# First tiles of a DFT kernel loaded in halves over two queues, with a shorter warm-up

## The chip, the cores and the metric

The kernel runs on one core of a Trainium2 chip. The core has five engines that run side by side, each with its own instruction stream: TensorE (matmuls, called PE in the profile; its weight loads are PEld), VectorE (DVE), ScalarE (ACT), GpSimd (POOL) and SyncE (SP). Loads from device memory are issued by an engine's queue, here SP's and ScalarE's, and carried by 16 DMA engines that all queues share. The metric is the device time of one execution in microseconds; 858.26 us is the median of three executions of the kernel before (858.01 to 858.42).

## The reference

For x of 2048 rows by 640 columns, the kernel mixes two results row by row with a gate g:

```python
g = sigmoid((x * gate_w).sum(-1, keepdims=True))
a = x @ dft_hid_re.T          # 2048 x 640
b = x @ dft_hid_im.T
A = dft_seq_re @ a - dft_seq_im @ b          # real part of the 2D DFT
h = x @ w1 + b1                              # 2048 x 1728
B = (h * tanh(softplus(h))) @ w2             # Mish
out = g * A + (1 - g) * B
```

All inputs and the output are 32-bit floats.

## The kernel before

The work is a long list of *steps*, written out when the kernel is built. A step loads tiles, prepares them, and runs matmuls on TensorE. Stages follow each other: the DFT along the sequence (`sq`), the DFT along the hidden dimension (`hd`), and the two dense products with Mish between them. Large products are cut into 2 by 2 blocks and done with seven block products in place of eight, so sums of tiles stand beside the matmuls.

Every 32-bit operand is split in two: a high part `h`, rounded to the format that TensorE reads fast, and a low part `l`, the rounding error. ScalarE makes the high part (`copy`, L144), VectorE the low part by a subtraction (`tt`, L141). A product is three matmuls: h with h, and each l with the other's h. All matmuls are issued in one helper (`mm`, L160).

The change touches the very start. The first stage multiplies c (`c_re`, a tile of 128 x 512, 256 KB, moving through TensorE) by x (`xn`, whose rows are stored in five blocks of 128 columns; the first three, a tile of 128 x 384 and 192 KB, are the weights here). Step 0 takes the first tile of each, c0 and x0, step 1 the second ones, and so on. Step 0 has its own preparation, `begin`, and its own order of matmuls, `products_by_part`:

```python
copy(wh, f[:, P:3 * P])                    # ScalarE: h of x0's blocks 1 and 2
for half in (LO, HI):
    nc.vector.tensor_copy(r[0][:, half], c[:, half])   # VectorE (L339): h of c0, by halves
tt(r[1], c, f32(r[0]), OP.subtract)        # VectorE: l of c0
tt(wl, f[:, P:3 * P], f32(wh), OP.subtract)
split(*part(w, 0, P), f[:, :P])            # h and l of x0's block 0
```

TensorE takes its matmuls in program order: c0's low half with x0's blocks 1 and 2, c0's high half with the same two, then all of c0 with block 0 (the *third product*), then the six with the low parts. ScalarE and VectorE are in order as well.

Loads of c and x are issued by the main loop on SP's queue (L1469), up to several steps ahead; tiles come from a pool of buffers (`FS`). Three things stand ahead of the loop: the loads of x0 and x1, issued on ScalarE's queue (L1351, L1353), the load of ScalarE's function table (L1354), and a warm-up of TensorE: `WARM` = 8 matmuls of 512 columns on a constant of ones, and one of 256 columns, whose results are not used. Each DMA tells of its landing through one of eight semaphores in turn, so an issue that takes a semaphore again waits for the landing of the DMA that had it.

Of the kernel before, what the change touches and what calls it, by code (L numbers as in the profile page):

```python
# [13 lines left out]
P = 128  # L14
# [5 lines left out]
FR = F - FC * P  # L20
NF = FC + 1
FP = 6
WARM = 8
EARLY = 3
LEAD = 8
LEAD_D = 5
# [80 lines left out]
def fnet_mish_gate(ctx: ExitStack, tc: tile.TileContext, xn, xt, c_re, c_im, wd_re, wd_im,  # L107
                   w1a, w1b, b1a, b1b, w2, gw, out):
    nc = tc.nc
# [48 lines left out]
    def mm(ps, a, b, start, stop):  # L158
        clock["pe"] += MM * ps.shape[-1] / N
        nc.tensor.matmul(ps, a, b, start=start, stop=stop, skip_group_check=True)  # L160
# [15 lines left out]
    LO, HI = slice(0, N // 2), slice(N // 2, N)  # L176
# [5 lines left out]
    def flush():  # L182
        while pend:
            pend.pop(0)()
# [38 lines left out]
    def job_load(i):  # L223
        j = jobs.pop(0)
        loaded.append((j, j.load(), i))

    def job_start():
        j, a, _ = loaded.pop(0)
        running.append((j.key, j.work(*a)))

    def job_go():
        key, work = running[0]
        pause = next(work, None)
        if pause is None:
            running.pop()
            done_jobs.add(key)
        return pause or 0
# [1110 lines left out]
        return f  # L1348

    x0 = RAW["xa", 0] = FS.get()  # L1350
    nc.scalar.dma_start(x0[:, :3 * P], xn[0, :, :3 * P])  # L1351
    x1 = RAW["xa", 1] = FS.get()
    nc.scalar.dma_start(x1[:, :3 * P], xn[1, :, :3 * P])  # L1353
    nc.scalar.preload_act_table_set("sigmoid_and_others")  # L1354
    ones = nc.const_aps.tensor(1.0, [P, N], F32).bitcast(F32R)
    for ps in psum.free[-WARM:]:
        mm(ps, ones[:, :P], ones, True, True)
# [94 lines left out]
    def spare(i, job=False):  # L1452

        return SPARE + (SPARE_D * job if i in narrow else (i >= n_dense) * SPARE_OUT) + sum(takes.get(i + j, 0) for j in range(5))

    li = ready = 0
    wait_until = 0
    for i in range(n_all):
        clock["step"] = i
        while ready < n_all and ready <= i + (LEAD_D if ready in narrow else LEAD):  # L1460
            while li < len(loads) and loads[li][0] <= ready + (AHEAD_D if loads[li][0] in narrow else AHEAD):
                n, (key, src) = loads[li]
                if n > ready and len(FS.free) <= spare(i):
                    break
                if id(src) in unwritten:
                    assert n > ready
                    break
                f = RAW[key] = FS.get()
                nc.sync.dma_start(f[:src.shape[0], :src.shape[1]], src)  # L1469
                li += 1  # L1470
            for prep in steps[ready][1]:
                prep()
            ready += 1
        clock["dve"] = max(clock["dve"], clock["pe"] - CREDIT)
        if not PEND or i + 1 not in narrow:
            flush()
        steps[i][2]()
        while stores and stores[0][3] <= i:
            dst, v, f, _ = stores.pop(0)
            nc.sync.dma_start(dst, v)  # L1480
            FS.put(f)
            unwritten.discard(id(dst))
        if steps[i][3]:
            steps[i][3]()
        for fn in events.get(i, ()):
            fn()
        if PEND == 1:
            flush()
        for r, w in list(extra) if i >= n_dense - BACK else ():
            if len(extra) > NB and any(r is o for o in R.free):  # L1490
                R.free = [o for o in R.free if o is not r]
                extra[:] = [e for e in extra if e[0] is not r]
                W.put(w)
        if i == 20:
            nc.sync.dma_start(b1s[:, :FC], b1a)
            nc.sync.dma_start(b1s[:FR, FC:], b1b)
        if not (jobs or loaded or running):
            while FX.free:
                FS.put(FX.get()[:, :N])
        while clock["dve"] < clock["pe"] + (SLACK_D if nd <= i < nm + D_END else SLACK if ("seq", "low", KH - 1) in done_jobs else SLACK_UP) and i >= wait_until and i not in quiet:  # L1500
            if running:
                wait_until = i + job_go()
            elif loaded and loaded[0][2] + (5 if i in narrow else 3) <= i and len(W.free) >= loaded[0][0].w:
                job_start()
            else:
                break
        while i not in no_load and jobs and len(loaded) < (NLOAD if i in narrow else 2) and len(FX.free) >= jobs[0].fx and i >= jobs[0].first and (i in narrow and not jobs[0].fs or len(FS.free) >= jobs[0].fs + spare(i, True)):
            job_load(i)
        if PEND == 2:
            flush()  # L1510
# [48 lines left out]
```

## Time and profile before

| | |
|---|---|
| median of three executions | 858.26 us (858.01 to 858.42) |
| the profiled execution, its own time | 857.84 us |
| its span, first to last instruction | 855.9 us |
| TensorE busy | 851.3 us, 99% of the span |
| VectorE, ScalarE busy | 87%, 59% |
| read from and written to device memory | 189.70 MB and 51.92 MB |

The page gives each engine's busy time. The chain of waits follows the work that ended last back to its start, and says at each step what released it. The timeline shows instructions in order of time: start, duration, engine, line, operation, output and inputs, and in brackets how long the engine was idle before and what ended that. A row of several merged instructions carries their number (x3). Names such as f, wh, rh and ps are the kernel's tiles: f for loaded tiles, rh and rl for the two parts of c, wh and wl for those of x, ps for accumulators.

### The profile page before, as it was taken

What the parts mean: (1) busy time and instruction counts of PE and PEld (TensorE: products, weight loads), DVE (VectorE), ACT (ScalarE), POOL (GpSimd) and SP (SyncE); (2) the same over time, 40 slices, a digit from 0 to 9 for tenths busy, and PEclk for the clock granted to TensorE, in tenths of its full rate; (3) what the DMA queues carried; (4) which work ended last, traced back from release to release, by engine and by line L of the source; (5) the groups of instructions that cost most, each with busy time, mean ns of one, the idle gap of its engine ahead of it and who ended that gap; (6) DMA issues with size and microseconds to landing.
All of it is one profiled execution on the core that took longest, in us unless ns stands there. A gap on an engine that the chain in (4) does not pass through costs nothing.

```text
span 855.9 us, 12423 instructions
## 1 busy us (share of the span) xinstructions
PE 851.3 (99%) x3748; PEld 704.3 (82%) x3748; DVE 742.0 (87%) x1320; ACT 507.0 (59%) x937; POOL 0.2 (0%) x4
## 2 busy tenths in 40 slices
PE   9999999999999999999999999999999999999998
PEld 7888888888888888888888888888888888888886
DVE  6999977999899869989898998877778889999991
ACT  6766646464555435757765665866867776542541
POOL 0000000000000000000000000000000000000000
PEclk9999999999999999999999999999999999999999
DMA  9975848594898999897677889999989997785942
GB/s 342 358 253 201 279 151 289 205 373 150 304 354 307 316 338 381 288 338 252 222 228 256 284 281 326 322 319 325 355 275 345 351 386 240 265 278 177 356 150 110
DMA packets 135602, 242.46 MB, mean 283 GB/s; under 512 B 15472, under 2 KB 22640, under 8 KB 135536
## 3 DMA queue, kind: packets, MB, share of 16 engines
q1 hardware_dynamic: 135104, 241.03, 82.0%
q8 instruction: 29, 0.48, 0.2%
q10 hardware_dynamic: 432, 0.66, 0.2%
q14 instruction: 37, 0.30, 0.1%
HBM read 189.70 MB, written 51.92 MB: 282 GB/s over the span
## 4 chain that ended last, share of the span: by engine, by line
PE 99%; DMA 0%; ACT 0%; issue 0%
PE ps L160 99%; DMA f<-in_xn_dram 0%; ACT f L144 0%; ACT wh L144 0%
## 5 line engine op out<-in xcount | busy, mean ns | idle before, releaser
L160 PE MATMUL ps<-rh,wh 128*128 128x512 f32 (+1 forms) x1029 | 398.7, 389 | 0.1
L160 PE MATMUL ps<-rl,wh 128*128 128x512 f32 x1017 | 394.7, 389 | 0.0
L160 PE MATMUL ps<-rh,wl 128*128 128x512 f32 x1016 | 394.3, 389 | 0.0
L144 ACT ACTIVATE rh<-f 128x512 fp32r<-128x512 f32 x420 | 255.5, 628 | 206.6 <-PE ps L160 101.3
L141 DVE TENSOR_TENSOR rl<-f,rh 128x512 fp32r<-128x512 f32 x419 | 281.5, 685 | 49.8 <-ACT rh L144 47.9
L141 DVE TENSOR_TENSOR f<-f,f 128x512 f32<-128x512 f32 (+2 forms) x342 | 218.6, 662 | 12.7 <-DMA u<-f 5.2
L160 PEld LDWEIGHTS ps<-rh,wh 128*128 128x128 f32 x1029 | 192.9, 188 | 40.6 <-ACT wh L144 0.6
L160 PEld LDWEIGHTS ps<-rl,wh 128*128 128x128 f32 x1017 | 190.9, 188 | 39.6
L160 PEld LDWEIGHTS ps<-rh,wl 128*128 128x128 f32 x1016 | 190.7, 188 | 39.5
L144 ACT ACTIVATE wh<-f 128x512 fp32r<-128x512 f32 (+3 forms) x201 | 91.8, 503 | 41.7 <-DVE f L141 33.7
L144 ACT ACTIVATE f<-ps 128x512 f32<-128x512 f32 (+1 forms) x135 | 77.2, 595 | 62.3 <-PE ps L160 52.4
L141 DVE TENSOR_TENSOR wl<-f,wh 128x512 fp32r<-128x512 f32 (+3 forms) x201 | 100.6, 535 | 9.8 <-ACT wh L144 9.4
L160 PE MATMUL ps<-wh,wh 128*128 128x512 f32 x232 | 90.3, 389 | 0.0
L160 PE MATMUL ps<-wh,wl 128*128 128x512 f32 x223 | 86.8, 389 | 0.0
L160 PE MATMUL ps<-wl,wh 128*128 128x512 f32 x222 | 86.4, 389 | 0.0
L141 DVE TENSOR_TENSOR f<-ps,f 128x512 f32<-128x512 f32 x98 | 63.5, 682 | 18.6 <-PE ps L160 17.9
L160 PEld LDWEIGHTS ps<-wh,wh 128*128 128x128 f32 x232 | 43.6, 188 | 9.1
L160 PEld LDWEIGHTS ps<-wh,wl 128*128 128x128 f32 x223 | 41.9, 188 | 8.7
L160 PEld LDWEIGHTS ps<-wl,wh 128*128 128x128 f32 x222 | 41.7, 188 | 8.6
L141 DVE TENSOR_TENSOR wl<-fx,wh 128x640 fp32r<-128x640 f32 (+2 forms) x43 | 28.4, 679 | 4.5 <-ACT wh L144 4.4
L144 ACT ACTIVATE wh<-fx 128x640 fp32r<-128x640 f32 (+4 forms) x46 | 27.5, 616 | 5.0 <-DVE fx L141 2.8
L141 DVE TENSOR_TENSOR f<-fx,f 128x256 f32<-128x256 f32 (+1 forms) x68 | 28.5, 442 | 1.5
(38 smaller groups left out, 171.0 us busy)
## 6 DMA issues: line engine op xcount, KB each, us to landing
f<-in_c_re_dram SPq DMA_DIRECT2D x128, 256.0 KB, 4.6
f<-in_c_im_dram SPq DMA_DIRECT2D x128, 256.0 KB, 5.0
f<-act SPq DMA_DIRECT2D x90, 256.0 KB, 4.9
f<-u SPq DMA_DIRECT2D x80, 256.0 KB, 3.8
f<-in_xt_dram SPq DMA_DIRECT2D x59, 256.0 KB, 4.8
act<-f SPq DMA_DIRECT2D x52, 256.0 KB, 4.2
u<-f SPq DMA_DIRECT2D x40, 256.0 KB, 4.5
f<-p SPq DMA_DIRECT2D x36, 256.0 KB, 4.6
```

Of the source, the lines that this page charges most:

```text
L141: nc.vector.tensor_tensor(o, a, b, op=op)
L144: nc.scalar.activation(o, a, AF.Copy, scale=scale)
L160: nc.tensor.matmul(ps, a, b, start=start, stop=stop, skip_group_check=True)
```

## The change

The warm-up loses one of its eight matmuls of 512 columns. c0 is loaded as two halves, the low one first on SP's queue, the high one second on ScalarE's. x0 is loaded as blocks 1 and 2, first on ScalarE's queue, and block 0, third there. x1 moves from ScalarE's queue to SP's, as its third load, behind c1. The table load stands behind ScalarE's three issues in place of two.

```diff
-WARM = 8
+WARM = 7
...
     x0 = RAW["xa", 0] = FS.get()
-    nc.scalar.dma_start(x0[:, :3 * P], xn[0, :, :3 * P])
+    nc.scalar.dma_start(x0[:, P:3 * P], xn[0, :, P:3 * P])
     x1 = RAW["xa", 1] = FS.get()
-    nc.scalar.dma_start(x1[:, :3 * P], xn[1, :, :3 * P])
-    nc.scalar.preload_act_table_set("sigmoid_and_others")
...
                 f = RAW[key] = FS.get()
-                nc.sync.dma_start(f[:src.shape[0], :src.shape[1]], src)
+                if li:
+                    nc.sync.dma_start(f[:src.shape[0], :src.shape[1]], src)
+                else:
+                    nc.sync.dma_start(f[:, LO], src[:, LO])
+                    nc.scalar.dma_start(f[:, HI], src[:, HI])
+                    nc.scalar.dma_start(x0[:, :P], xn[0, :, :P])
+                    nc.scalar.preload_act_table_set("sigmoid_and_others")
                 li += 1
+                if li == 2:
+                    nc.sync.dma_start(x1[:, :3 * P], xn[1, :, :3 * P])
```

Here `li` counts the loads of the list, so `li` = 0 is c0. ScalarE's stream at the start of the program, before; f_91 is x0, f_92 x1, f_93 c0, f_94 c1, f_95 c2 and f_96 x2, and DMAHWn is the n-th of the eight semaphores:

```order
L1351 DMA f_91<-in_xn_dram 128x384
L1353 DMA f_92<-in_xn_dram 128x384
L1354 ACT_TABLE_LOAD
L144 ACTIVATE wh_117<-f_91 128x256 [waits DMAHW0_49]
L144 ACTIVATE wh_117<-f_91 128x128
L144 ACTIVATE rh_75<-f_94 128x512 [waits DMAHW3_49]
L144 ACTIVATE wh_119<-f_92 128x384 [waits DMAHW2_49]
```

and the same place after the change:

```order
L1351 DMA f_91<-in_xn_dram 128x256
L1471 DMA f_93<-in_c_re_dram 128x256
L1472 DMA f_91<-in_xn_dram 128x128
L1473 ACT_TABLE_LOAD
L144 ACTIVATE wh_117<-f_91 128x256 [waits DMAHW0_49]
L144 ACTIVATE wh_117<-f_91 128x128 [waits DMAHW4_49]
L144 ACTIVATE rh_75<-f_94 128x512 [waits DMAHW3_49]
L144 ACTIVATE wh_119<-f_92 128x384 [waits DMAHW5_49]
```

The rounding of x0's block 0 (128x128), which had no wait of its own, now waits for a transfer of its own, and the roundings of c1 and x1 stand behind it. SP's queue at the start of the program, before:

```order
L1469 DMA f_93<-in_c_re_dram 128x512
L1469 DMA f_94<-in_c_re_dram 128x512
L1469 DMA f_95<-in_c_re_dram 128x512
L1469 DMA f_96<-in_xn_dram 128x384
L1469 DMA f_97<-in_c_re_dram 128x512
L1469 DMA f_98<-in_xn_dram 128x384
L1469 DMA f_99<-in_c_re_dram 128x512 [waits DMAHW0_49]
L1469 DMA f_100<-in_xn_dram 128x384 [waits DMAHW1_49]
L1469 DMA f_101<-in_c_re_dram 128x512 [waits DMAHW2_49]
```

and after the change:

```order
L1470 DMA f_93<-in_c_re_dram 128x256
L1468 DMA f_94<-in_c_re_dram 128x512
L1476 DMA f_92<-in_xn_dram 128x384
L1468 DMA f_95<-in_c_re_dram 128x512
L1468 DMA f_96<-in_xn_dram 128x384
L1468 DMA f_97<-in_c_re_dram 128x512 [waits DMAHW0_49]
L1468 DMA f_98<-in_xn_dram 128x384 [waits DMAHW1_49]
L1468 DMA f_99<-in_c_re_dram 128x512 [waits DMAHW2_49]
```

x1 (f_92) now stands third, c2 and all loads behind it one place later, and the first issue that waits for a landing is c3's (f_97) and no longer c4's (f_99). VectorE's stream changes in two waits: the cast of c0's high half and the subtraction for x0's block 0 each have a semaphore of their own now. TensorE's stream loses one warm-up matmul.

## The prediction

> **What bounds the kernel now.** I read the page's busy rows first, then the chain that ended last, then the first 8 us in order of time.
>
> ```profile
> PE 851.3 (99%) x3748; PEld 704.3 (82%) x3748; DVE 742.0 (87%) x1320; ACT 507.0 (59%) x937; POOL 0.2 (0%) x4
> ...
> PE 99%; DMA 0%; ACT 0%; issue 0%
> ```
>
> TensorE is busy for 851.3 of 855.9 us. Nothing that another engine does counts, unless it moves TensorE's start. The first pieces of the chain, in order of time, say where the start is set:
>
> ```profile
> 0.72 3.56 DMA f<-in_xn_dram
> 4.28 0.02 issue
> 4.31 0.43 ACT wh L144
> 4.73 0.04 issue
> 4.78 25.28 PE ps L160 x112
> ```
>
> x's first tile takes from 0.72 to 4.28 to land, ScalarE rounds two of its three blocks in 0.43, and from 4.78 TensorE runs matmuls without a gap (25.28 / 112 = 0.226 us each). All that this change can win or lose lies ahead of that. The same place in the timeline (start, duration, engine, line, what):
>
> ```profile
> 1.64 1.28 ACT L1354 ACT_TABLE_LOAD   x1 [1.64 <-PEq L1547]
> 4.12 0.29 DVE L339 CAST rh<-f 128x256 fp32r<-128x256 f32 x1 [4.12 <-DMA f<-in_c_re_dram]
> 4.63 0.29 ACT L144 ACTIVATE wh<-f 128x128 fp32r<-128x128 f32 x1
> 4.65 0.69 DVE L141 TENSOR_TENSOR rl<-f,rh 128x512 fp32r<-128x512 f32 x1
> 4.78 0.39 PE L160 MATMUL ps<-rh,wh 128*128 128x256 f32 x1
> 5.00 0.52 PE L160 MATMUL ps<-rh,wh 128*128 128x256 f32 x3
> 5.23 0.63 ACT L144 ACTIVATE rh<-f 128x512 fp32r<-128x512 f32 x1 [0.30 <-DMA f<-in_c_re_dram]
> 5.26 0.62 DVE L141 TENSOR_TENSOR wl<-f,wh 128x256 fp32r<-128x256 f32 x2
> 5.36 0.40 PE L160 MATMUL ps<-rh,wh 128*128 128x512 f32 x1
> 5.40 0.33 SPq L1469 DMA_DIRECT2D f<-in_c_re_dram  x1
> 5.59 0.39 PE L160 MATMUL ps<-rl,wh 128*128 128x512 f32 x1
> 5.76 0.51 ACT L144 ACTIVATE wh<-f 128x384 fp32r<-128x384 f32 x1
> 6.99 0.39 PE L160 MATMUL ps<-rh,wh 128*128 128x512 f32 x1
> 7.57 0.64 ACT L144 ACTIVATE rh<-f 128x512 fp32r<-128x512 f32 x1 [0.17 <-DMA f<-in_c_re_dram]
> ```
>
> c's first tile is there at about 4.10 (cast at 4.12) and its second at 5.21 (ScalarE starts at 5.23). x's second lands at about 5.38, for SP's issue at 5.40 waits on that transfer's semaphore. TensorE does four half matmuls from 4.78, the third product (x's block 0) at 5.36, and step 1 begins at 6.99. That third product is the row to watch: it needs x0[:, :P], which the change puts last on ScalarE's queue.
>
> **How fast the first bytes come.** The windows of the start (window, length, the five engines' busy time, granted clock, DMA share, GB/s), and the packets of each queue in 0.8 us of it (q1 is SP's, q10 ScalarE's):
>
> ```profile
> 1.50:2.50 1.00, 1.00 (x4) 0.82 (x3) 0.00 (x0) 0.86 (x1) 0.00 (x0) 1.00 0.71 95
> 2.50:3.00 0.50, 0.50 (x2) 0.36 (x2) 0.00 (x0) 0.43 (x1) 0.00 (x0) 1.00 0.87 313
> 3.00:3.50 0.50, 0.50 (x3) 0.38 (x2) 0.00 (x0) 0.00 (x0) 0.00 (x0) 1.00 1.05 398
> 3.50:4.00 0.50, 0.50 (x3) 0.41 (x2) 0.00 (x0) 0.00 (x0) 0.00 (x0) 1.00 1.06 403
> 4.00:4.40 0.40, 0.40 (x3) 0.23 (x1) 0.28 (x2) 0.09 (x1) 0.00 (x0) 1.00 1.06 405
> 4.40:4.80 0.40, 0.28 (x3) 0.03 (x1) 0.36 (x3) 0.40 (x2) 0.00 (x0) 1.00 1.12 342
> ...
> q1 hardware_dynamic: 111, 0.20, 64.6%
> q10 hardware_dynamic: 90, 0.12, 41.3%
> ```
>
> Added up, 95 kB have moved by 2.5, 252 by 3.0, 451 by 3.5, 652 by 4.0, 814 by 4.4 and 951 by 4.8. The engines are full from 3.0 on, so order decides. Between 3.5 and 4.3 the queues moved 111 and 90 packets, though q10's are 1.5 KB and q1's 2 KB: they take turns by packet, not by byte. The first pair of tiles (262 + 197 = 459 kB) is reached at 3.52, and lands at 4.10 (SP) and 4.28 (ScalarE); both pairs together (918 kB) at 4.70, landing at 5.21 and 5.38. From "moved" to "landed" is thus 0.5 to 0.6 us on SP's queue and 0.7 to 0.8 on ScalarE's.
>
> **The change part by part.** *Halves, by the same sums.* The first pair is now c0's low half and x0's blocks 1 and 2, 131 kB each: 262 kB at 3.03, landing at 3.6 and 3.80, half a microsecond earlier. Second on ScalarE's queue is c0's high half, and it takes turns with all of c1, which follows on SP: 128 packets beside 128, so it is through when 262 + 131 + 262 = 655 kB are, at 4.0, and lands at 4.77 instead of 4.10. Third is x0's block 0 (66 kB), beside x1 (197 kB): through at 918 kB, the same 4.70 as before, landing at 5.40 instead of 4.28. More packets for the same bytes add a little. Loads of 1 KB rows elsewhere show their price, against a stretch of 2 KB packets (q1 in 3 us around 414, and from 4.9 to 5.4):
>
> ```profile
> q1 hardware_dynamic: 576, 0.52, 58.9%
> ...
> q1 hardware_dynamic: 87, 0.17, 91.1%
> ```
>
> That is 0.589 x 16 x 3 / 576 = 49 ns, against 0.911 x 16 x 0.5 / 87 = 84 ns, so two halves cost 98 where one whole cost 84; with 8 rows for each DMA engine c0 takes 0.11 us longer, x0 about as much or less. x0's block 0 then lands at 5.5. The bounds are 5.4 (packets free) and 5.7 (0.2 for packets; and 0.1 if the slow packets up to 2.5 are no faster for being small, for then some 40 to 50 kB of the 95 are still to move, at 400 GB/s).
>
> *TensorE's start.* The wide rounding ends at 3.80 + 0.02 + 0.42, and the two low halves can start at 4.29, which is 0.49 earlier. That gain is not kept. The high half is cast from 4.79 to 5.08, its two matmuls start at about 5.13 and are over by 5.5. The third product waits for 5.5 + 0.02 + 0.29 (ScalarE's 128x128 row) + 0.05 (from 4.73 to 4.78, as now) + 0.10 (the first matmul after an empty pipe took 4.78 to 5.00, the next ones 0.12) = 5.96. Before it started at 5.36. **Sum: +0.60 us**, bounds +0.50 and +0.80; the early start is swallowed by the two waits behind it.
>
> *What stands behind the new wait.* TensorE takes its work in order, so all of step 0 is behind it. ScalarE too: c1's rounding waits behind block 0's, to 5.81 + 0.63 = 6.44, then x1's to 6.95; step 1 wants them at 6.99 + 0.60 = 7.59. VectorE: the rounding error of c0 comes at 5.08 + 0.69 = 5.8 (wanted 6.19), x0's two by 6.5 (wanted 6.88). So nothing else is late.
>
> *Half a microsecond less warm-up.* One matmul fewer at 0.43 (below) ends it at about 4.1 instead of 4.5. Taken at nothing: TensorE waits for data then anyway; the cover is the wait to 4.29. *Table load:* behind three issues instead of two (0.45 more) it runs from 2.09 to 3.37, 0.4 ahead of the first rounding: nothing. If it took over 0.4 longer, the low halves would start late, and still ahead of block 0. *SP's queue:* x1 takes the third place, c2 and all behind it move on by one, and c3's issue now waits for x0's landing (3.80; before it went at 2.58). c3 is wanted at 6.99 + 2 x 2.04 = 11.1 (nine matmuls of 0.226 a step), and it was there at 7.57, 3.5 us ahead; the issue moves by 1.2: nothing.
>
> [...]
>
> **Rivals.** *Turns by byte.* If small packets let ScalarE's queue through sooner, c0's high half is through at 524 kB (3.68, landing 4.45) and block 0 at 655 kB (4.0, landing 4.77); the third product starts at 5.23, 0.13 us earlier: 858.1. The 111 against 90 packets speak against it. Break-even is a landing of block 0 at about 4.9.
>
> *The half speed lasts longer.* Warm-up and end of the kernel:
>
> ```profile
> 3.03 1.06 PE L160 MATMUL ps<-const-float32-1.0 128*128 128x512 f32 x2
> 3.46 1.06 PE L160 MATMUL ps<-const-float32-1.0 128*128 128x512 f32 x2
> 3.89 0.77 PE L160 MATMUL ps<-const-float32-1.0 128*128 128x512 f32 x2
> ...
> 850.90:854.30 3.40, 1.33 (x6) 0.75 (x5) 0.00 (x0) 1.19 (x2) 0.00 (x0) 1.00 0.63 238
> 854.40:855.90 1.50, 0.00 (x0) 0.00 (x0) 0.00 (x0) 0.00 (x0) 0.00 (x0) 0.50 0.04 12
> ```
>
> Warm-up matmuls follow each other in 0.43 us, real ones of the same size in 0.23: TensorE runs at half speed at first, though the clock column reads 1.00 there, and it has full speed by 5.0, some 3.5 to 4.2 us after it began at 0.77. At the end, 3.4 us with 1.33 us of work took it to 0.50. After the change the work is broken from 4.1 to 4.29, from 4.65 to 5.13 and from 5.5 to 5.96. If these gaps make the count begin again at 5.96, half speed lasts 3.5 to 4.2 us longer and costs half of that, 1.75 to 2.1, beyond the 0.6: 860.6 to 861.0, slower by 0.3%. Against it speaks that the gap from about 4.5 to 4.78 did no harm, and that the work from 0.77 to 4.65 would be nine tenths busy. The mechanism decides from the point where the switch misses its place near 4.5. [...]
>
> **How the numbers follow.** The sum stands against the profiled execution, 857.84 us (855.9 and 1.9 around it), which gives 858.44; the median shown is 0.42 higher, and 858.26 + 0.60 gives 858.9. Late block 0: 0.70. Turns by byte, or anything that lands block 0 by 4.9: 0.16. Half speed lasting: 0.11. The rest, 0.03, is unexplained. The range goes from 858.26 - 0.13 - 0.25 (down to the lowest run) = 857.9 to 858.26 + 0.80 + 0.58 (from the profiled to the highest run) = 859.6, leaving out the half speed. 0.2% is 1.7 us, about what a measurement of this kernel can tell from no change. No start can win that much, as TensorE waits only until 4.78 and the clock's switch lies at 4.3 or later: faster 0.02. Slower is the half speed: 0.11. Same: 0.87.
>
> **What would show it.** Right: the chain of waits names x's block 0 on ScalarE's queue; the first real matmul is near 4.3, the third product near 6.0, step 1 near 7.6; ScalarE waits again for in_xn ahead of its 128x128 rounding. Wrong: the third product before 5.36 (turns by byte); real matmuls 0.43 apart after 6.0 (half speed); new idle time on TensorE behind 8 us (SP's order mattered after all).

## The result, and the profile after

The changed kernel takes 860.84 us (median of seven executions, 858.78 to 862.0), against 858.01 us (857.33 to 858.42, seven as well) for the kernel before. The ratio is 1.0033, with a 95% interval of 1.0021 to 1.0044: slower by a third of a percent. The profiled execution took 860.84 us, its span is 859.0, which is 3.1 more than before.

The busy row of the page after:

```profile
PE 852.9 (99%) x3747; PEld 705.4 (82%) x3747; DVE 742.5 (86%) x1320; ACT 507.6 (59%) x937; POOL 0.2 (0%) x4
```

TensorE is idle for 6.1 us in place of 4.6 (859.0 - 852.9, 855.9 - 851.3): 1.5 more. It is also busy for 1.6 us more, with one matmul fewer. So there are two losses: TensorE waits longer, and it works more slowly somewhere. The chain of waits of the kernel after, its first pieces (start, duration, what), shows where the first one is:

```profile
0.73 0.41 ACTq L1351
...
1.16 0.46 ACTq L1471
...
1.65 4.61 DMA f<-in_xn_dram
...
6.28 0.32 ACT wh L144
...
6.64 23.45 PE ps L160 x95
```

ScalarE's queue issues x0's blocks 1 and 2 (L1351), c0's high half (L1471), and then x0's block 0, which lands at 6.26, 4.61 us after its issue. ScalarE rounds it, and TensorE goes on at 6.64. The timeline of the same place:

```profile
3.24 0.29 DVE L339 CAST rh<-f 128x256 fp32r<-128x256 f32 x1 [3.24 <-DMA f<-in_c_re_dram]
3.43 0.42 ACT L144 ACTIVATE wh<-f 128x256 fp32r<-128x256 f32 x1
4.10 0.47 PE L160 MATMUL ps<-rh,wh 128*128 128x256 f32 x2
4.41 0.29 DVE L339 CAST rh<-f 128x256 fp32r<-128x256 f32 x1 [0.88 <-DMA f<-in_c_re_dram]
4.75 0.50 PE L160 MATMUL ps<-rh,wh 128*128 128x256 f32 x2 [0.18 <-DVE rh L339]
6.28 0.31 ACT L144 ACTIVATE wh<-f 128x128 fp32r<-128x128 f32 x1 [2.44 <-DMA f<-in_xn_dram]
6.50 0.62 ACT L144 ACTIVATE rh<-f 128x512 fp32r<-128x512 f32 x1
6.64 0.50 PE L160 MATMUL ps<-rh,wh 128*128 128x512 f32 x1 [1.39 <-ACT wh L144]
6.98 0.91 PE L160 MATMUL ps<-rl,wh 128*128 128x512 f32 x3
7.68 1.49 PE L160 MATMUL ps<-rh,wl 128*128 128x512 f32 x3
8.96 0.63 PE L160 MATMUL ps<-rh,wh 128*128 128x512 f32 x1
```

The first halves are there early, as they were meant to be: the cast of c0's low half at 3.24, the wide rounding of x0 at 3.43, the first real matmul at 4.10 in place of 4.78. Then TensorE waits 1.39 us for block 0. The third product starts at 6.64; before, it started at 5.36: 1.28 later. The last rows show the second loss. The three matmuls from 6.98 take 0.23 us each, from start to start ((7.68 - 6.98) / 3), and the three from 7.68 take 0.43 ((8.96 - 7.68) / 3). The windows of this stretch (window, length, busy time of TensorE, its weight loads, VectorE, ScalarE and GpSimd, the granted clock, DMA share, GB/s), after:

```profile
4.24:7.65 3.41, 1.84 (x9) 1.28 (x8) 2.12 (x5) 1.37 (x4) 0.00 (x0) 1.00 0.99 346
7.66:11.06 3.40, 3.40 (x9) 2.67 (x8) 3.40 (x8) 3.40 (x8) 0.00 (x0) 0.50 1.02 378
11.07:11.20 0.13, 0.13 (x2) 0.11 (x1) 0.13 (x1) 0.13 (x1) 0.00 (x0) 1.00 0.85 323
```

and before:

```profile
4.24:7.65 3.41, 3.29 (x16) 2.50 (x15) 3.37 (x9) 2.83 (x7) 0.00 (x0) 1.00 1.03 360
7.66:11.06 3.40, 3.40 (x16) 2.81 (x15) 2.84 (x6) 2.73 (x6) 0.00 (x0) 1.00 1.05 380
```

The trace's record of the granted clock begins at 4.24, with full speed; ahead of its first entry the column reads 1.00 too, although the warm-up matmuls there follow each other in 0.43 us and the real ones of the same size from 6.98 in 0.23. From 7.65 to 11.07 the record has 0.50, and then 1.00 again. TensorE does 9 matmuls in that time where it did 16. Half of 3.4 us is lost: 1.7. In the same length of time ahead of it TensorE had been busy for 1.84 of 3.41 us; before the change, for 3.29. Together 1.28 + 1.7 = 2.98 of the 3.1 us.

That is the profiled execution, and it doesn't stand for all of them. A stretch of 3.41 us at 0.50 lowers an execution's mean granted clock by 0.002. Of the six executions above 860 us, three have a mean of 0.997 or 0.998 (860.84, 861.05, 861.12). The other three (860.51, 860.59, 862.0) have 0.999 or 1.000, as the kernel before has: there the clock was not taken back. The experiments show a second way to lose the same time, full speed that comes late, at 10.23 to 13.22 in four profiles.

### The profile page after: what moved, and what is told of

It is laid out like the page before. It is cut to its first block, busy times and chain, and to the rows that moved or that the text cites. A ratio compares the mean times of both kernels' runs of the same rounds, so it can differ in the third digit from the quotient of the medians.

```text
span 859.0 us, 12424 instructions
## 1 busy us (share of the span) xinstructions
PE 852.9 (99%) x3747; PEld 705.4 (82%) x3747; DVE 742.5 (86%) x1320; ACT 507.6 (59%) x937; POOL 0.2 (0%) x4
## 4 chain that ended last, share of the span: by engine, by line
PE 99%; DMA 1%; ACT 0%; ACTq 0%; issue 0%
PE ps L160 99%; DMA f<-in_xn_dram 1%; ACT f L144 0%; ACTq L1471 0%; ACTq L1351 0%; ACT wh L144 0%
```

## The experiments

Two things had to be told apart: what takes the clock away (the gap in front of block 0, or the shorter warm-up), and why block 0 lands at 6.26 and not at 5.5. Of the fourteen kernels seven start from the changed kernel and seven from the kernel before. None leaves computation out; some add work whose result nobody reads, as said with each. The kernel before, run beside them, took 857.69 to 857.90 us (medians); each ratio is against it, and follows the means of all executions rather than the medians. The times given below at which full speed came are the first entries in the traces' records of the granted clock.

### The warm-up at its old length

```diff
-WARM = 7
+WARM = 8
```

> The changed kernel with the eighth warm-up matmul put back, all else as changed. Theory (late block, then the clock): block 0 of x's first tile still lands near 6.2, TensorE still stands idle for over 1 us ahead of the third product, and the clock still falls to half for some 3.4 us afterwards: 860.8, within 0.4. Rival (the shorter warm-up lost the clock): full speed is held from the start, and only the late block is left: about 859.1.

860.69 us (eleven executions), ratio 1.0023 (1.0014 to 1.0032). The executions fall into two groups with nothing between them: five from 858.72 to 858.82 and six from 860.69 to 861.14. The profiled execution, 858.81, is of the lower group. Its chain and two of its windows:

```profile
1.65 4.19 DMA f<-in_xn_dram
5.84 0.02 issue
...
6.22 5.97 PE ps L160 x25
```

```profile
2.90:6.32 3.42, 2.94 (x10) 2.20 (x9) 1.73 (x5) 1.39 (x4) 0.00 (x0) 1.00 1.03 375
...
6.32:9.73 3.41, 3.41 (x15) 2.86 (x16) 3.18 (x7) 3.41 (x8) 0.00 (x0) 1.00 1.06 388
```

In this execution block 0 landed at 5.84 and the third product started 0.86 late (6.22 - 5.36). Full speed came at 6.32 (10 matmuls in the first window, 15 in the second), it stayed, and 0.9 us were lost in all (858.81 - 857.90). So this group pays about what the late block costs. The upper one lies some 2 us higher, about the price of 3.4 us at half clock (1.7). No profile fell in it, but the mean granted clock of all six is 1.000. So the fall to half that I had expected happened in none of the eleven; that full speed came a stretch late in the six is argued from the distance and the clock. The changed kernel has the same two groups: 858.78 once, and six from 860.51 to 862.0. Five of eleven against one of seven is too few to say that the warm-up's length changes the odds. And with the old warm-up the median is as high, so the matmul that was taken out isn't needed for the jump.

### Warm-up matmuls in the gap

Six matmuls of 512 columns on the constant of ones, results not read, in front of the third product of the changed kernel:

```diff
+        if first:
+            pe = clock["pe"]
+            for _ in range(6):
+                mm(psum.free[-1], ones[:, :P], ones, True, True)
+            clock["pe"] = pe
```

> The changed kernel with six matmuls of 512 columns on ones, whose results nobody reads, put between the high half's matmuls and the third product; no load is touched. Theory (late block, then the clock): the third product stays at about 6.6, but TensorE is busy until it, the clock is not taken back, and real matmuls follow each other in 0.23 us from there on: 860.8 - 1.7 = 859.1. Rival (everything comes from waiting for data; the clock plays no part): 860.8, or a little more.

859.54 us (859.14 to 860.05, eleven executions), ratio 1.0018 (1.0009 to 1.0026). The timeline and two windows:

```profile
5.41 1.70 PE L160 MATMUL ps<-const-float32-1.0 128*128 128x512 f32 x6
...
6.94 0.40 PE L160 MATMUL ps<-rh,wh 128*128 128x512 f32 x1
7.18 0.86 PE L160 MATMUL ps<-rl,wh 128*128 128x512 f32 x3
```

```profile
4.40:7.60 3.20, 3.12 (x13) 2.50 (x13) 2.21 (x5) 1.45 (x4) 0.00 (x0) 1.00 1.02 365
7.70:11.00 3.30, 3.30 (x16) 2.73 (x15) 3.30 (x7) 3.29 (x8) 0.00 (x0) 1.00 1.02 361
```

The third product starts at 6.94, later than without the filling (6.64), and still the kernel is 1.3 us faster: full speed comes at 5.86 and stays, and no execution is above 860.05. More work in the gap costs less than the gap. This is the run that shows that the second loss hangs on TensorE's idle time.

### The same gap without any change of the loads

To have the gap alone: the kernel before, in which ScalarE rounds a constant, unread, ahead of x0's block 0. Three roundings in the first kernel, four in the last; the second has three roundings and the six matmuls of above in the gap.

```diff
+        for n in (N, N, P):
+            copy(psum.free[-2][:, :n], ones[:, :n].bitcast(F32))
```

> The kernel before with three roundings of a constant on ScalarE (128x512 twice, 128x128; results unread) ahead of the rounding of block 0. No load is changed; the third product is held up to about 6.4 to 6.9 as in the changed kernel. Theory (late block, then the clock): 1.1 to 1.6 us of waiting, and in most runs 1.7 us of half speed on top: 860 to 861.5 in the median. Rival (the loads themselves cost the rest of the 2.8 us): only the wait, 859.0 to 859.6 in all runs.

> As f2 with six matmuls on ones between the high half's matmuls and the third product. Theory: the wait stays, the clock is held: 859.0 to 859.7, in a narrow band. Rival (half speed comes from something else than TensorE's idle time): as f2.

> As the kernel with ScalarE held up by three roundings of a constant, with a fourth (128x512, 0.63 us). No load is changed; the third product moves from about 6.0 to about 6.6, as in the changed kernel, and TensorE's idle time ahead of it grows from 0.4 to about 1.0 to 1.2 us. Theory (a long enough gap loses the clock): the runs fall into two groups 1.7 to 2 us apart, near 859.2 and near 861, and more of them than 2 in 11 lie in the upper one. Rival (the clock is lost only where the loads are as in the changed kernel): one group near 859.2.

With three roundings the gap came out at only 0.42 us: the third product started at 6.01. 858.72 us, ratio 1.0015 (1.0006 to 1.0024); nine executions from 858.59 to 858.87, two at 860.46 and 860.49. The median I had expected is missed, since the gap was too short. Filled with matmuls the same kernel took 859.08 us (858.9 to 860.0), ratio 1.0016 (1.0007 to 1.0025): no execution jumped, but the median is 0.36 higher, so a gap this short wasn't worth filling. With four roundings it took 859.56, ratio 1.003 (1.0017 to 1.0042): four executions from 859.47 to 859.60, one at 860.8, one at 862.49. The profiled one is of the lower four. Its third product in the timeline, and two windows:

```profile
6.98 0.50 PE L160 MATMUL ps<-rh,wh 128*128 128x512 f32 x1 [1.09 <-ACT wh L144]
```

```profile
4.40:7.60 3.20, 2.11 (x9) 1.47 (x8) 1.56 (x5) 3.10 (x8) 0.00 (x0) 1.00 1.06 389
7.70:11.00 3.30, 3.30 (x17) 2.69 (x16) 3.30 (x7) 3.30 (x8) 0.00 (x0) 1.00 1.04 375
```

A gap of 1.09 us, nearly that of the changed kernel, and the clock stayed: full speed had come at 5.73, and in the 3.41 us from there TensorE was busy for 2.32. So a gap may bring the second loss, but needn't: 2 of 11 executions jumped in the kernel whose profile shows 0.42 us, 2 of 6 in the one with 1.09 us, none of 11 with the 0.42 filled, and 1 of the 118 executions of the kernel before (860.62). These counts are small. The jump, 1.7 us in the first kernel (860.48 - 858.72), needs no changed load. The mean clock of the four that jumped is 1.000, so full speed wasn't taken back in them; that it came late is argued, as no profile fell in them.

### Low parts ahead of block 0

The changed kernel, with step 0's matmuls in another order: the products of the low parts with blocks 1 and 2 go first, and the three of block 0 last, so that TensorE has work while block 0 is under way.

```diff
+        if first:
+            for n, c in ((0, l), (1, h)):
+                for ps, w in todo[:2]:
+                    mm(ps, w[n], c, False, False)
+            ps, w = todo[2]
+            for n, c, start in ((0, h, True), (0, l, False), (1, h, False)):
+                mm(ps, w[n], c, start, False)
+            return
```

> The changed kernel with step 0's matmuls in another order: the low parts of c and x with blocks 1 and 2 ahead of the three products with block 0, so that real work stands in the gap; loads as changed. Theory (late block, then the clock): the gap shrinks from 1.4 to 0.3 to 0.5 us, the clock is held, step 1 begins at 7.3 to 7.6 and not at 8.5 or later: 858.2 to 858.9 and no second group 1.7 us above. Rival (late loads cost in later steps too, whatever step 0 does): 860 or more.

859.33 us (858.36 to 860.5, eleven executions), ratio 1.0016 (1.0007 to 1.0025): 1.5 us better than the changed kernel, 0.4 above the expected range, and still not as good as the kernel before. In the profiled execution (860.49, among the highest) block 0 landed at 6.53 and held nobody up, but the matmuls were still at half speed at 7.6, as its timeline shows:

```profile
5.02 0.79 PE L160 MATMUL ps<-rh,wh 128*128 128x256 f32 x2 [0.29 <-DVE rh L339]
...
7.62 0.63 PE L160 MATMUL ps<-rh,wh 128*128 128x512 f32 x1
...
8.05 0.63 PE L160 MATMUL ps<-rl,wh 128*128 128x512 f32 x1
```

Full speed came only at 10.23 here, and was not taken back. The idle time left was 0.29 us ahead of c0's high half.

### The warm-up cut alone

The kernel before, with `WARM = 7`.

> The kernel before with WARM = 7, nothing else. Theory (late block, then the clock): the warm-up ends at 4.1, TensorE idles 0.7 us until 4.78, and the clock is held: 858.0, within 0.3. Rival (the shorter warm-up lost the clock): half speed lasts a window longer: about 859.7.

858.00 us (857.35 to 858.63, eleven executions), ratio 1.0000 (0.9991 to 1.0009). Nothing: the 1.7 us of one more stretch of 3.41 us at half speed are in no execution.

### Block 0 ahead of c0's high half

```diff
-                    nc.scalar.dma_start(f[:, HI], src[:, HI])
                     nc.scalar.dma_start(x0[:, :P], xn[0, :, :P])
+                    nc.scalar.dma_start(f[:, HI], src[:, HI])
```

> The changed kernel with the second and third issue on ScalarE's queue exchanged: block 0 of x's first tile ahead of c's high half. Theory (late block, then the clock): block 0 lands near 4.2, c's high half at 4.5 to 4.9, the third product starts at 5.2 to 5.5, no gap is over 0.6 us, the clock is held: 857.8 to 858.4. Rival (the shorter warm-up lost the clock): the order of loads gives back only the 1.3 us of waiting: about 859.6.

Missed by about 4 us: 862.03 (860.41 to 862.64, five executions), ratio 1.0047 (1.0034 to 1.006). Block 0 did land early, at 4.51. But c0's high half, now third, landed at 6.94. The chain, and the row of the timeline that waits for it:

```profile
1.66 5.28 DMA f<-in_c_re_dram
6.94 0.02 issue
```

```profile
7.32 1.23 PE L160 MATMUL ps<-rh,wh 128*128 128x256 f32 x3 [2.58 <-DVE rh L339]
...
10.90 1.48 PE L160 MATMUL ps<-rh,wh 128*128 128x512 f32 x3
12.18 1.04 PE L160 MATMUL ps<-rl,wh 128*128 128x512 f32 x3
13.06 0.39 PE L160 MATMUL ps<-rh,wl 128*128 128x512 f32 x1
```

So the place is slow, not the tile. The third load on SP's queue, x1, landed as late, at 6.76. With this gap of 2.58 us half speed lasted long: TensorE did 10 matmuls from 7.7 to 11.0, where the kernel before does 16. Here full speed was not taken back; it had not come yet. It came at 12.57: the three matmuls from 10.90 are 0.43 apart, those from 12.18 only 0.29. In two of the five executions (861.59, 862.03) the mean clock is 0.997, as in the changed kernel's profile, which speaks for a stretch taken back there.

### x1 one place later on SP's queue

In the changed kernel, `li == 3` in place of `li == 2`: x1 is loaded behind c2. This asks whether x1's bytes beside block 0 hold it up.

> The changed kernel with x's second tile one place later on SP's queue, behind c's third, so that block 0 has c's third tile beside it and not x's second. Theory P (the third place on ScalarE's queue is late whatever stands beside it): block 0 lands at 5.8 or later, the gap ahead of the third product is over 0.9 us, 860.5 within 0.5. Rival X (the rows of x's second tile are slow and hold block 0 up): block 0 lands by 5.6, the third product starts by 6.1, 858.8 to 859.5.

862.03 us (860.77 to 862.5, four executions), ratio 1.0044 (1.0029 to 1.0059). Block 0 landed at 6.71, and the third product waited 1.29 us for it, in the timeline:

```profile
7.10 0.79 PE L160 MATMUL ps<-rh,wh 128*128 128x512 f32 x1 [1.29 <-ACT wh L144]
```

Not earlier, but later. So x1's bytes beside it don't make block 0 late. The landing and the gap are as Theory P had them; the median is 1 us above its range, and in the profiled execution (862.5) full speed came only at 13.22.

### c0 on one queue, x0 on the other

Both halves of c0 on SP's queue, both parts of x0 and then x1 on ScalarE's, so that step 0 needs no third place. The second kernel has `WARM = 8` besides.

```diff
-                    nc.scalar.dma_start(f[:, HI], src[:, HI])
+                    nc.sync.dma_start(f[:, HI], src[:, HI])
                     nc.scalar.dma_start(x0[:, :P], xn[0, :, :P])
+                    nc.scalar.dma_start(x1[:, :3 * P], xn[1, :, :3 * P])
...
-                if li == 2:
-                    nc.sync.dma_start(x1[:, :3 * P], xn[1, :, :3 * P])
```

> Halves in the order of need: SP's queue carries c's first tile as low half and high half, ScalarE's carries x's first tile as blocks 1 and 2, then block 0, then x's second tile. Theory P: both second halves land in the second place of their queues, by 4.5, real matmuls begin at 3.9 and no gap is over 0.5 us; x's second tile, now in third place, lands at 5.4 to 6.2, and step 1 waits at most 0.5 us for it: 857.4 to 858.2, the kernel before or a little faster. Rival (any split into halves costs, by more and smaller packets): block 0 later than 5, 859 or more.

> As e6 with the eighth warm-up matmul put back. TensorE is in the warm-up until 4.3 to 4.5 and starts the real matmuls up to 0.4 us later at half speed, where 0.4 us is worth 0.2: 857.6 to 858.3, equal to e6 within 0.3. Rival (the warm-up length sets the clock): faster than e6 by 1 us or more in the median.

858.75 us (858.39 to 859.32) and 858.68 us (858.49 to 859.44), eleven executions each, ratios 1.0011 (1.0002 to 1.0019) and 1.001 (1.0001 to 1.0019). Better than the changed kernel by 2.1 us, and in no execution the jump; but the gain that I had expected didn't come. The halves were all there early (ScalarE's two roundings of x0 run from 3.62, and the second cast of c0 starts at 3.97), and then the third places were late again: c1 on SP's queue landed at 6.42, and step 1 waited. Of the first kernel's chain:

```profile
1.64 4.78 DMA f<-in_c_re_dram
...
7.54 4.60 PE ps L160 x19
```

Step 1 starts at 7.54, against 6.99 before: all the start gained, and 0.55 more, went to the third place. In the profile of the second kernel c1 landed at 7.43, and TensorE stood idle for 1.74 us ahead of step 1, the longest gap of all in which the clock stayed. Counted in steps of 3.41 us from the coming of full speed, which is an estimate, it lay across the end of a step, and in the two steps TensorE was busy for 2.26 and 2.82 us.

### c0 alone in halves

The kernel before, with c0 alone cut, its high half second on ScalarE's queue and x1 third there.

> The kernel before with only c's first tile in halves: the low one first on SP's queue, the high one second on ScalarE's; x's first tile whole and first, x's second third on ScalarE's queue, warm-up of eight and a half. Theory P: x's first tile lands at 3.7 to 4.1 whole, the high half by 4.7, both second at worst; the one in third place is x's second tile (5.5 to 6.3), which step 1 wants at 6.4: 857.8 to 858.6. Rival (the split of c, not block 0, costs): 859.5 or more.

858.82 us (858.24 to 860.0, eleven executions), ratio 1.0013 (1.0005 to 1.0022). Missed as well: x1, third, landed at 7.27, and step 1 started at 7.87 in the timeline:

```profile
7.87 0.96 PE L160 MATMUL ps<-rh,wh 128*128 128x512 f32 x3 [0.37 <-ACT wh L144]
```

### Is it the number of loads?

Two loads of 128 rows of 16 bytes, 4 KB together, unread, in the kernel before: in the first kernel both on ScalarE's queue between x0 and x1, in the second one at the head of each queue.

```diff
+    for i in range(2):
+        tiny = sb.tile([P, 4], F32, name=f"tiny{i}")
+        nc.scalar.dma_start(tiny, xn[2 + i, :, :4])
```

```diff
+    tiny = [sb.tile([P, 4], F32, name=f"tiny{i}") for i in range(2)]
+    nc.scalar.dma_start(tiny[0], xn[2, :, :4])
+    nc.sync.dma_start(tiny[1], xn[3, :, :4])
```

> The kernel before with two loads of 128 rows by 16 bytes (4 KB in all, into buffers that nobody reads) on ScalarE's queue between x's first and second tile. Theory C (what counts at the start is the number of loads, each of which takes its time to be set up, whatever its bytes): x's second tile, now the fourth load of its queue, lands 0.4 to 1.5 us later than 5.4, and DMA bandwidth dips between 3.5 and 5; 858.0 to 858.9. Rival (bytes and turns alone, as the prediction reckoned): it lands at 5.4 to 5.5, and the time is that of the kernel before within 0.2 us.

> The kernel before with one load of 128 rows by 16 bytes (into a buffer that nobody reads) ahead of everything on each of the two queues. Theory Q (each queue only needs its issue time): the first tiles land 0.45 us later, c's at about 4.2 to 4.55 and x's at 4.4 to 4.75, 858.2 to 858.5. Rival S (loads of both queues are set up one after the other, each taking some 0.4 us whatever its bytes): 0.8 us later or more, 858.6 to 859.

The first took 858.55 us (858.26 to 858.83), ratio 1.0008 (0.9998 to 1.0017). With 4 KB ahead of it, x1 landed at 6.74 in place of 5.38, and c2, on the other queue, at 5.68 in place of 6.18. x1's rounding in the timeline:

```profile
6.76 0.53 ACT L144 ACTIVATE wh<-f 128x384 fp32r<-128x384 f32 x1 [1.36 <-DMA f<-in_xn_dram]
```

So the queues take turns by packet even when one's packets hold 16 bytes: each of the 256 small rows let a row of 2 KB pass. Between 3.5 and 5.05 ScalarE's queue moved 279 packets (0.02 MB) and SP's 283 (0.50 MB). The 5.4 to 5.5 that the expectation gives for x1 was reckoned wrong; by turns x1 is through only when c0 and x0 (459 kB), c1 and c2 (262 each), and x1 with an equal load beside it (394) have moved. TensorE had no gap, and no execution jumped. In the profile full speed came at 6.68, and step 1 began at 7.69; how much of the 0.9 us over the kernel before is x1's stays open.

The second took 858.5 us, ratio 1.0014 (1.0005 to 1.0023), in two groups: six from 858.1 to 858.52 and four from 860.45 to 860.89. c0 landed at 4.71 and x0 at 4.88, against 4.10 and 4.28 in the profile before (and 3.65 and 3.85 in the earliest profile with the same loads, that of the three roundings). The profiled execution is the highest (860.89); its timeline:

```profile
5.37 1.65 PE L160 MATMUL ps<-rh,wh 128*128 128x256 f32 x5 [0.64 <-ACT wh L144]
6.82 1.48 PE L160 MATMUL ps<-rl,wh 128*128 128x512 f32 x3
8.10 1.48 PE L160 MATMUL ps<-rh,wl 128*128 128x512 f32 x3
```

A gap of 0.64 us in front of the first real matmul, and step 0 ran through at half speed ((8.10 - 6.82) / 3 = 0.43); full speed came at 10.24. The landings speak for a cost of each load at a queue's head, the lower group's times against a large one; the run doesn't settle it.

## Why the prediction was wrong

**The early start: right.** The chain names x's block 0 on ScalarE's queue, ScalarE waits for it ahead of its 128x128 rounding, and the early halves bring nothing. They came even earlier than said: the wide rounding started at 3.43 (3.80 + 0.02 in the working), c0's high half was cast at 4.41 (4.79). Both are 0.4 early. Most of that is the profile that the working stood on: in the five profiles with the loads of the kernel before, x0 lands between 3.85 and 4.28, and that one has the latest. Turns by byte would have brought block 0 early too, and it wasn't.

**Block 0's landing: right in kind, mis-sized.** The term was a landing at 5.5, bounds 5.4 and 5.7, and +0.60 us. Measured were 6.26 and +1.28; 5.84 and +0.86 with the long warm-up, 6.71 with x1 moved. The working took the engines as full from 3.0 on, and then only order decides. They weren't. The windows of the changed kernel:

```profile
3.50:4.00 0.50, 0.50 (x3) 0.40 (x2) 0.03 (x1) 0.35 (x1) 0.00 (x0) 1.00 1.23 262
4.00:4.40 0.40, 0.40 (x4) 0.37 (x2) 0.00 (x0) 0.00 (x0) 0.00 (x0) 1.00 0.63 173
4.40:4.80 0.40, 0.22 (x3) 0.05 (x1) 0.36 (x2) 0.00 (x0) 0.00 (x0) 1.00 0.93 222
4.80:5.20 0.40, 0.40 (x2) 0.25 (x2) 0.40 (x1) 0.00 (x0) 0.00 (x0) 1.00 0.77 275
```

Where the kernel before moved 403, 405, 342 and 332 GB/s, it is now 262, 173, 222 and 275: 234 kB less in 1.7 us, 0.6 us at 400 GB/s. The block was 0.76 later than said, so the sag would explain most of it, but not all: with the long warm-up the rate stayed at 365 or more over these windows, and the block was still 0.34 late. With c0 on one queue the sag is deepest, in the same view,

```profile
3.50:4.00 0.50, 0.50 (x3) 0.27 (x1) 0.24 (x2) 0.38 (x1) 0.00 (x0) 1.00 0.82 199
4.00:4.40 0.40, 0.38 (x3) 0.31 (x3) 0.37 (x2) 0.29 (x2) 0.00 (x0) 1.00 0.52 106
```

and with c0 alone cut there is none (397, 363, 353, 328 GB/s), though its third load came at 7.27. The sag is not the whole of it. The trace's packet records show what is behind the rest: every load there ends with 16 packets of 4 bytes, and it had landed 0.4 to 0.55 us after the last of them. For x0 in the kernel before these come between 3.27 and 3.79. For block 0 with the long warm-up fifteen come from 4.65 to 4.80, as the sum had it (moved at 4.70), and the last at 5.47; by then 1207 kB had moved in place of 918. In the changed kernel they come from 4.51 to 5.88, with 1230 kB moved. So the sixteen parts of these loads didn't keep step, the last part decided, and later loads went past it. The step of the sum that failed is "order decides": it took the bytes to arrive in one order on all sixteen engines. Both queues are held up alike: the third load on SP's landed within 0.3 us ahead of the third on ScalarE's in every kernel that has one. What holds single parts back stays open. It isn't x1's bytes (6.71 with x1 moved), nor the tile (6.94 for c0's high half in the same place), nor the warm-up (5.84 with the old one); rows of 16 bytes bring only a small sag (355, 320, 319 and 343 GB/s).

The price of packets was read a little too high: the counts hold the packets of 4 bytes as well. A row of 1 KB took 46 ns and one of 2 KB 84, so two halves cost 92, not 98. That made nothing late.

**The half speed: the rival that came true, at a chance of 0.11.** Its total, 860.6 to 861.0, holds the measured 860.84, and its price beyond the late block, 1.75 to 2.1, is near the 1.7 seen. That the total fits is partly luck, as it has 0.60 for the late block, which cost 1.28, and stands on 858.26, where the kernel before now took 858.01. The step that failed is the place of the switch. I took full speed to come near 4.5, from one profile, and argued that the switch would not be missed there: a gap from 4.5 to 4.78 had done no harm, and the work up to 4.65 would be nine tenths busy. In the sixteen profiles it has no such place. Full speed came between 3.70 and 6.68 in twelve of them, the kernel before at 4.45, and at 10.23, 10.24, 12.57 and 13.22 in the other four, each with a gap before it. The step after it failed as well, as I did not ask whether full speed could be taken back. In the profiled execution of the changed kernel it came at 4.24, and was. The row for that stood in the working: at the kernel's end, 3.4 us with 1.33 us of work, and then 0.50. With the late block the gap grew from the 0.46 of the forecast (5.5 to 5.96) to 1.39 us, and 1.84 of 3.41 us busy came near that row. So the first error fed the second; how often 0.46 alone would have done it is left open by the two of eleven with 0.42.

The traces' records show more of when the clock changes. In that of the changed kernel the first stretch at full speed and the one at 0.50 behind it last 3.413 us each. From its last coming to its end full speed lasted 846.5 us there, 849.9 in the kernel before, and in the other profiles one of the two or 853.3: 248, 249 or 250 times 3.413. Its first coming differs by up to 3 us between the twelve profiles that have it early. From these numbers I take the clock to change in steps of 3.41 us, which lie differently against the program's start from one execution to the next; that is an estimate. By it the same gap can fall into different parts of a step, and keep full speed from coming (four profiles), take it back (one), or do neither. That this alone parts a kernel's times into groups is argued, not shown. How long a gap must be to lose the clock is not shown either: 1.39 us lost it in the changed kernel's profile, and 1.74 us didn't with c0 on one queue and the old warm-up.

**What cost nothing: right.** The shorter warm-up (858.00 against 857.90), the table load (2.13 to 3.41, the rounding starts at 3.43, which is closer than the 0.4 I had reckoned, as the halves came early), and SP's order: after 6.64 the chain is TensorE alone. ScalarE's c1 and x1 were rounded by 7.12 and 7.53, ahead of step 1 at 8.96.

## What to carry to other kernels

A start that waits once is cheaper than one that begins early and waits in the middle: beside its own length, a wait near the start cost 1.7 us in the profile of the changed kernel, half of 3.4 us at half clock, because full speed was taken back, and in four other profiles it came late. So fill a long one with matmuls (1.3 us won here with six in a gap of 1.39 us; 0.36 lost in one of 0.42), or order the work so that the late piece is needed last (1.5 us). A start that was profiled once shows one place of the clock's change of several (4.45 in the kernel before, 3.70 to 6.68 over twelve profiles); look at the spread of the executions too. Before a tile is cut to have its first part early, ask what its last part will wait for: in each kernel here that cut the first tiles, a load in the third place of its queue came late, at 5.84 to 7.43, and gave the gain back. No kernel of this study was faster than the one before.

## What the runs showed of the hardware

- In the record of the changed kernel the granted clock was 1.00 for 3.41 us, 0.50 for 3.41 us, and then 1.00 for 846.5. Full speed came first at 3.70 to 6.68 us in twelve profiles, and at 10.23 to 13.22 in four with a gap. The stretch ahead of the 0.50 was 54% busy (1.84 of 3.41 us). Steps of 3.41 us counted from the first coming of full speed (an estimate, as the record has no entry between them) with 2.26 and 2.32 us busy were not followed by 0.50. Full speed came after 3.41 us with 2.9 us busy (the long warm-up) and didn't after a step with 3.1 (low parts first; the ends of matmuls are modelled), so the busy time of the records doesn't give the rule.
- The column of the granted clock reads 1.00 at the start of the program, ahead of the first entry in the trace's record, while matmuls follow each other in 0.43 us. The mean clock of an execution counts that time as 1.00 too: the 0.999 of the kernel before is what its last 1.5 us, at 0.50, take off (1.5 x 0.5 / 855.9 = 0.0009). Only the distance of matmuls shows the speed at the start.
- The two queues took turns by packet down to 16 bytes (279 and 283 packets from 3.5 to 5.05): 4 KB in such rows held up the load behind them by 1.36 us (6.74 - 5.38).
- x0's block 0, 66 kB and third on its queue, landed between 5.84 and 6.71 in the five kernels that load it there and were profiled, where bytes and turns give 5.5. It had landed 0.4 to 0.55 us after the last of its 16 parts, and one part was late by itself with the long warm-up (5.47, with the other fifteen through by 4.80). In some of these kernels the rate of all 16 DMA engines together sagged; the lowest window was 106 GB/s, with c0 on one queue.
